# Hedgehog linear attention with a gated Mish layer on one core: one half-piece of w1, the kv product and Q's subtraction moved within the seven-product chunks

## The chip, the cores and the metric

The kernel runs on one NeuronCore of one Trainium2 chip. TensorE (PE) multiplies matrices, VectorE (DVE) does element work and reductions, ScalarE (ACT) does activations and copies, GpSimd (POOL) does element work and starts some DMAs, SyncE (SP) starts most of the others. Each engine runs its own instructions in order and waits on semaphores of the others. The metric is the device time of the program in microseconds (us).

## The reference, cut to what matters

```python
qkv = x @ wqkv                                   # x: 2048 x 512; q, k, v: 32 heads of 16
pq, pk = q @ w_phi, k @ w_phi                    # per head
phi = concat(softmax(p), softmax(-p))            # for q and k
kv, z = phi_k^T v, sum_s phi_k                   # per head
a = ((phi_q kv) / (phi_q z + 1e-6)) @ wo
b = mish(x @ w1 + b1) @ w2                       # 512 -> 1376 -> 512
out = g * a + (1 - g) * b,  g = sigmoid(x . gate_w)
```

## The kernel before

The 2048 rows of x are cut into eight chunks (0 to 7) of 256 rows, two tiles of 128 each. Phase A runs over the chunks and makes, for each tile t, K with w_phi folded in (`k`), V (`v`) and Q (`q`), the feature map E of K, and adds up kv = E^T v in one PSUM tile and z = sum of E. Q goes to DRAM (`pqd`) and is read again in phase B. Phase B then runs over four blocks of 512 rows: the Mish layer (`up`, `down`), Q's features, the numerator (`nu`), wo and the output.

Every float32 operand of a large product is split into a high part (an ACT copy to fp32r, step `H`, `xh`, `sh`) and a low part (a subtraction, step `O`, `xl`, `sl`), and a product is high*high + high*low + low*high. w1 and w2 are loaded and split in phase A in twelve numbered pieces, 1024 columns wide but for pieces 5 and 11 (512): `Lj` starts the load of piece j (line 165, on SP), `Hj` is ACT's copy, `Oj` POOL's subtraction (line 517). Raw pieces share two buffers, so `Lj` waits for the `O` two loads back: L5 for O3, L7 for O5, L8 for O11, L9 for O7.

A chunk as a rule takes 72 matmuls of 128x512. Chunks 3, 4 and 5 (`FAST`) take 66: K and Q of two tiles are a 2x2 block product, done with seven half-size products (`s1` to `s7`, six matmuls each) in place of eight, plus 24 matmuls for V. Their operands are combinations of x's blocks, made one chunk ahead: `sa` (four POOL additions, line 335), `sh0`/`sl0` (for s7 and s6) and `sh1`/`sl1` (for s5 and s3; lines 342 and 343). The tiles with the raw combinations are called sraw; their split parts lie for now in w2b's tiles, and the split combinations of the weights in w2a's and w2b's, so that w2ah or w2bh in the profile's "proj" products are these operands. In PE's order a chunk is s1, s7, s2, s6, v0, s4, s5, v1, s3. ACT copies s1's result into Q's PSUM tile (`bc`) and s7's into SBUF (`m7`). DVE adds them into the second K's PSUM tile (`ca`, line 381), upon which s4 accumulates; after s5, DVE subtracts the second tile's Q out of the same PSUM tile (`qa`, line 420), and only then may s3 go on accumulating there. qa's result goes to DRAM by `st1`.

The feature map of tile t on DVE: maxima and minima of each head (`mx`, `mn`, line 262), two subtractions (`d0`, `d1`, lines 269 and 271), ACT's exponential (`E`), sums (`S`, line 277), reciprocals (`rS`, line 285) and the scaling E*1/S (`ml`, line 293). Then E goes to `z` (chunks 0 to 4: an accumulating DMA that POOL starts, line 445; later an addition on POOL, line 443), and both tiles of two chunks go to kv together (`kk`, 64 small matmuls a chunk): chunks 2 and 3 in chunk 4's time, 4 and 5 in chunk 6's. `xh`, `xl` split the next chunk's x, `ldx` loads the one after that.

The order of all steps is written out by hand as strings of step names: `SEVEN` for chunks 3 to 5, `NEXT` for 6, `LAST` for 7, `BLOCK0` and on for phase B. `run` emits steps in that order, and each engine keeps the order in which its instructions are emitted. A trailing ' means the previous chunk's step, + the next one's, # a weight piece. In SEVEN the words `more` and `rest` stand for weight pieces and differ by chunk. POOL's `O` steps and the first addition of `sa` are made to wait for the DVE step emitted last, by hand:

```python
def behind(ins, other=None):
    tc.add_manual_dep(ins.ins, (other or dve[0]).ins.name, SYNC, reason="VectorE's step first")
...
            behind(pin(G_.tensor_sub(l[:, cs], raws[j], f32(h[:, cs]))))
```

where `dve[0]` is the last `xl` or `ml` so far.

Of the kernel before, what the change touches and what calls it, by code (L numbers as in the profile page):

```python
# [49 lines left out]
    v1 H1# S1 rS1 ml1 l3# O1# L3# ve1 q0 qe0 st0 q1 qe1 st1  # L50
"""
SEVEN = """
    s1 bc s7 m7 kk s2 xh xl zld sa z1' more mx0 mn0 s6 ca d00 d10 E0 ldx v0 ve0 sh0 sl0 za rest S0 rS0 s4 mx1 mn1 s5 qa st1 d01 d11 E1 ml0 z0
    v1 S1 rS1 s3 ve1 qe0 st0 ml1 sh1 sl1
"""
NEXT = """
    lq0+ k0 xh xl z1' mx0 mn0 k1 kk d00 d10 ldx H9# E0 O9# ldw0 L10# mx1 mn1 d01 d11 H6# E1 O6# ldw1 S0 rS0 ml0 z0 v0 ve0 H10#
# [37 lines left out]
def tile_gated_mix(ctx: ExitStack, tc: tile.TileContext, xT, wv, wkT, wqT, bd, w1a, w1b, b1, w2a, w2b, wo, out):  # L95
# [109 lines left out]
    def run(text, key, prev=None, nxt=None):  # L205
        for w in text.split():
            k = prev if w.endswith("'") else nxt if w.endswith("+") else "W" if w.endswith("#") else key
            for fn in steps.pop((k, w.rstrip("'+#")), ()):
                fn()
# [664 lines left out]
    run(SECOND, ("A", 1), ("A", 0))  # L874
    run(BEFORE, ("A", 2), ("A", 1))
    for c in FAST:
        w = {3: ("", "H2# O2# L4# H3# O3# L5#"), 4: ("", "H4# O4# L11# H5# O5# L7#"), 5: ("H11# O11# L8# H7# O7# L9#", "H8# O8# L6#")}[c]
        run(SEVEN.replace("more", w[0]).replace("rest", w[1]), ("A", c), ("A", c - 1))
    for c, text in ((NCH - 2, NEXT), (NCH - 1, LAST)):
        run(text, ("A", c), ("A", c - 1), ("B", 0))  # L880
    for b in range(NB):
# [62 lines left out]
```

## Time and profile before

| what | value |
|---|---|
| median of 3 runs | 453.68 us (449.16 to 454.94) |
| the profiled execution's own time | 454.35 us |
| its span in the profile | 452.3 us |
| PE busy / DVE busy / ACT / POOL | 442.9 / 318.9 / 209.4 / 161.9 us |
| chunk 3, from s1 to the next s1 | 64.81 to 80.45 us |
| chunk 4 | 80.45 to 101.77 us |
| chunk 5 | 101.77 to 116.73 us |
| phase B starts | 153.89 us |

The profile is of one execution; its times are counted from the start of the span. A row of the timeline gives the start, the length, the engine, the line of the code, the operation with the tile written and the tiles read, and in brackets the idle time of the engine ahead of it and what ended that. The own time is 2.05 us longer than the span, which is what lies around it.

### The profile page before, as it was taken

To read this page: it belongs to the slowest core of one execution; us is meant where nothing else is said; L and a number is where in the kernel's file an instruction comes from. 1 tells how busy PE (TensorE), PEld (TensorE's weight loads), DVE (VectorE), ACT (ScalarE), POOL (GpSimd) and SP (SyncE) were. 2 spreads that over 40 slices of the span, in tenths; PEclk is the share of its full clock that TensorE was granted. 3 is DMA by queue.
4 is the path that set the end of the run, shared out by engine and by line. 5 is a ranking of instruction groups with operands and counts; after the bars stand their busy time and mean duration, and the time that the engine had idled before them with its cause. 6 is when DMAs were issued, how large, how long until landed. Compare 5 with 4: busy or idle time off the path is not lost.

```text
span 452.3 us, 7013 instructions
## 1 busy us (share of the span) xinstructions
PE 442.9 (98%) x2754; PEld 361.3 (80%) x2754; DVE 318.9 (71%) x423; ACT 209.4 (46%) x289; POOL 161.9 (36%) x116
## 2 busy tenths in 40 slices
PE   7999999799999999999999999999999999999996
PEld 7888887688888888878787887887887888787885
DVE  2499778887899999799989976576967529611002
ACT  5774554445445565726265444534253553243220
POOL 2296757667495455221122212023212122221211
PEclk9999999999999999999999999999999999999999
DMA  7426756748955200413434150331151302030002
GB/s 279 164 82 203 162 113 166 185 100 224 275 201 154 73 24 1 99 43 87 146 94 141 30 156 32 92 112 47 30 136 58 94 13 93 1 84 11 0 0 93
DMA packets 27320, 46.35 MB, mean 102 GB/s; under 512 B 5908, under 2 KB 14100, under 8 KB 27288
## 3 DMA queue, kind: packets, MB, share of 16 engines
q1 hardware_dynamic: 25528, 39.88, 28.7%
q0 software_dynamic: 1616, 5.77, 6.7%
q8 instruction: 21, 0.34, 0.3%
q10 hardware_dynamic: 144, 0.26, 0.2%
q14 instruction: 11, 0.09, 0.1%
HBM read 23.87 MB, written 13.64 MB: 83 GB/s over the span
## 4 chain that ended last, share of the span: by engine, by line
PE 93%; DVE 4%; DMA 1%; issue 1%; ACT 0%; DVEq 0%; ACTq 0%
PE up L107 27%; PE down L107 26%; PE proj L107 25%; PE wo L107 10%; PE num L107 2%; PE fuse L107 2%; PE kvp L107 1%; DVE E L293 1%; DMA wT<-in_wkT_dram 1%; DVE Sm L277 1%; DVE io L788 0%; DVE mx L262 0%; DVE E L271 0%; DVE E L269 0%; DVE mn L262 0%
## 5 line engine op out<-in xcount | busy, mean ns | idle before, releaser
L653 POOL TENSOR_TENSOR l<-act,h 128x512 fp32r<-128x512 f32 x44 | 60.3, 1370 | 219.9 <-ACT h L127 184.2
L127 ACT ACTIVATE act<-up,b1s 128x512 f32<-128x512 f32 x44 | 30.3, 688 | 88.8 <-PE up L107 88.7
L127 ACT ACTIVATE E<-E 128x1024 f32<-128x1024 f32 x32 | 33.6, 1060 | 51.4 <-DVE E L271 31.2
L293 DVE TENSOR_TENSOR E<-E,Sm 128x1024 f32<-128x1024 f32 x32 | 46.4, 1451 | 1.0
L277 DVE TENSOR_REDUCE Sm<-E 128x64 f32<-128x1024 f32 x32 | 38.7, 1211 | 7.8 <-ACT E L127 7.8
L107 PE MATMUL wo<-woh,ohl 128*128 128x512 f32 x128 | 40.7, 389 | 0.0
L107 PE MATMUL down<-w2ah,h 128*128 128x512 f32 x96 | 37.5, 390 | 0.0
L107 PE MATMUL down<-w2ah,l 128*128 128x512 f32 x96 | 37.4, 389 | 0.0
L107 PE MATMUL down<-w2al,h 128*128 128x512 f32 x96 | 37.3, 389 | 0.0
L788 DVE SCALAR_TENSOR_TENSOR io<-down,og_sb,io 128x512 f32<-128x512 f32 x16 | 11.2, 749 | 31.0 <-PE down L107 31.0
L107 PE MATMUL down<-w2bh,h 128*128 128x512 f32 x80 | 31.2, 390 | 0.0
L107 PE MATMUL down<-w2bl,h 128*128 128x512 f32 x80 | 31.1, 389 | 0.0
L107 PE MATMUL down<-w2bh,l 128*128 128x512 f32 x80 | 31.1, 389 | 0.0
L127 ACT ACT_TABLE_LOAD x20 | 25.7, 1283 | 10.1 <-PE up L107 9.8
L762 DVE TENSOR_TENSOR ohl<-num,ohl 128x512 fp32r<-128x512 f32 x16 | 10.2, 679 | 26.3 <-ACT ohl L127 26.3
L127 ACT ACTIVATE h<-act 128x512 fp32r<-128x512 f32 x44 | 27.8, 632 | 1.4
L107 PEld LDWEIGHTS wo<-woh,ohl 128*128 128x128 f32 x128 | 24.0, 188 | 5.1
L107 PE MATMUL up<-xbh,w1ah 128*128 128x512 f32 x96 | 26.2, 394 | 0.0
L107 PE MATMUL up<-xbh,w1al 128*128 128x512 f32 x96 | 25.7, 389 | 0.0
L107 PE MATMUL up<-xbl,w1ah 128*128 128x512 f32 x96 | 25.7, 389 | 0.0
L107 PE MATMUL wo<-wol,ohl 128*128 128x512 f32 x64 | 24.9, 389 | 0.0
L550 DVE TENSOR_TENSOR xbl<-xraw,xbh 128x1024 fp32r<-128x1024 f32 x8 | 10.0, 1287 | 19.8 <-ACT xbh L127 19.8
(156 smaller groups left out, 1014.8 us busy)
## 6 DMA issues: line engine op xcount, KB each, us to landing
xraw<-in_xT_dram SPq DMA_DIRECT2D x16, 512.0 KB, 4.5
eT<-tt SPq DMA_DIRECT2D x128, 64.0 KB, 2.0
zd<-E POOLq DMA_DIRECT2D x10, 512.0 KB, 6.0
pqd<-qs SPq DMA_DIRECT2D x16, 256.0 KB, 4.0
pq<-pqd SPq DMA_DIRECT2D x16, 256.0 KB, 2.9
out_dram<-io SPq DMA_DIRECT2D x16, 256.0 KB, 2.1
raw<-in_w1a_dram SPq DMA_DIRECT2D x3, 512.0 KB, 4.5
raw<-in_w2a_dram SPq DMA_DIRECT2D x3, 512.0 KB, 4.2
```

Source lines behind the costliest of these rows:

```text
L107: return pin(nc.tensor.matmul(*a, **k))
L127: return pin(A_.activation(out_, in_, fn, **k))
L277: pin(V.tensor_reduce(d["S"], hv(d["E"][:, :]), axis=AX.X, op=ALU.add))
L293: dve[0] = pin(eng.tensor_mul(hv(d["E"][:, :]), hv(d["E"][:, :]), d["S"][:, :, None].to_broadcast([P, 2 * H, DH])))
L550: dve[0] = pin(V.tensor_sub(xb[b][1][:, :, sl], kt(raw[h], SC), f32(xb[b][0][:, :, sl])))
L653: pin(G_.tensor_sub(U[i]["l"], U[i]["a"], f32(U[i]["h"])))
L762: pin(V.tensor_sub(ohl[h, gp][:, 512:], num[h, gp], f32(ohl[h, gp][:, :512])))
L788: pin(V.scalar_tensor_tensor(io[t], dn[t], og_sb[:, i : i + 1], io[t], op0=ALU.mult, op1=ALU.add))
```

## The change

In the words of the strings: SEVEN's `kk` moves from behind m7 to behind s6 (it does something in chunk 4 alone); `qa st1` moves ahead of `mx1 mn1` in chunks 3, 4 and 5 (s5, a PE step, comes with it in the text, and PE's own order stays); and a new word `late` at the end of the string takes the second weight piece of the middle of the chunk: in chunk 3 `O3 L5`, in chunk 4 `O5 L7`, in chunk 5 nothing. H3 and H5, ACT's copies, stay where they were. Since `late` follows ml1, the DVE step that O3 and O5 wait for by hand is now ml1, the second scaling, and no longer the xl or ml0 of before. No instruction is added or taken away.

```diff
 SEVEN = """
-    s1 bc s7 m7 kk s2 xh xl zld sa z1' more mx0 mn0 s6 ca d00 d10 E0 ldx v0 ve0 sh0 sl0 za rest S0 rS0 s4 mx1 mn1 s5 qa st1 d01 d11 E1 ml0 z0
-    v1 S1 rS1 s3 ve1 qe0 st0 ml1 sh1 sl1
+    s1 bc s7 m7 s2 xh xl zld sa z1' more mx0 mn0 s6 kk ca d00 d10 E0 ldx v0 ve0 sh0 sl0 za rest S0 rS0 s4 s5 qa st1 mx1 mn1 d01 d11 E1 ml0 z0
+    v1 S1 rS1 s3 ve1 qe0 st0 ml1 sh1 sl1 late
 """
...
-        w = {3: ("", "H2# O2# L4# H3# O3# L5#"), 4: ("", "H4# O4# L11# H5# O5# L7#"), 5: ("H11# O11# L8# H7# O7# L9#", "H8# O8# L6#")}[c]
-        run(SEVEN.replace("more", w[0]).replace("rest", w[1]), ("A", c), ("A", c - 1))
+        w = {3: ("", "H2# O2# L4# H3#", "O3# L5#"), 4: ("", "H4# O4# L11# H5#", "O5# L7#"), 5: ("H11# O11# L8# H7# O7# L9#", "H8# O8# L6#", "")}[c]
+        for name, part in zip(("more", "rest", "late"), w):
+            text = (SEVEN if name == "more" else text).replace(name, part)
+        run(text, ("A", c), ("A", c - 1))
```

PE at the start of chunk 4, before: proj_870 is s7, kvp are the kv products of chunk 2 (E_608, E_641) and chunk 3 (E_778, E_833), proj_869 is s2, proj_877 is s6.

```order
L107 MATMUL proj_870<-w2ah_128,w2bl_131 128x512 x2
L107 MATMUL kvp_537<-E_608,v_668 32x64 x16
L107 MATMUL kvp_537<-E_641,v_694 32x64 x16
L107 MATMUL kvp_537<-E_778,v_797 32x64 x16
L107 MATMUL kvp_537<-E_833,v_861 32x64 x16
L107 MATMUL proj_869<-wkh_118,xh_753 128x512 x2
L107 MATMUL proj_869<-wkl_119,xh_753 128x512 x2
L107 MATMUL proj_869<-wkh_118,xl_755 128x512 x2
L107 MATMUL proj_877<-w2ah_128,w2bh_130 128x512 x2
```

And after, where E_830 is the second E of chunk 3 and proj_989 is v0:

```order
L107 MATMUL proj_869<-wkh_118,xl_755 128x512 x2
L107 MATMUL proj_877<-w2ah_128,w2bh_130 128x512 x2
L107 MATMUL proj_877<-w2al_129,w2bh_130 128x512 x2
L107 MATMUL proj_877<-w2ah_128,w2bl_131 128x512 x2
L107 MATMUL kvp_537<-E_608,v_668 32x64 x16
L107 MATMUL kvp_537<-E_641,v_694 32x64 x16
L107 MATMUL kvp_537<-E_778,v_797 32x64 x16
L107 MATMUL kvp_537<-E_830,v_858 32x64 x16
L107 MATMUL proj_989<-wvh_120,xh_752 128x512 x2
```

The 64 small products of kv (the profile counts two records for each) now stand behind s2 and s6.

POOL from the middle of chunk 3 to chunk 4's end, before: raw_692 is piece 3 (O3), raw_803 piece 4, raw_809 piece 5 (O5); w2bl is written by sl1, sl0 and sl1; zd are the accumulating DMAs; sraw_965<-xraw is sa.

```order
L517 TENSOR_TENSOR w1al_659<-raw_662,w1ah_658 128x1024
L517 TENSOR_TENSOR w1bl_806<-raw_692,w1bh_805 128x1024
L445 DMA zd_124<-E_778 128x1024
L343 TENSOR_TENSOR w2bl_131<-sraw_760,w2bh_130 128x512
L335 TENSOR_TENSOR sraw_965<-xraw_782 128x256 x2
L335 TENSOR_TENSOR sraw_965<-xraw_782,sraw_965 128x256 x2
L445 DMA zd_125<-E_833 128x1024
L343 TENSOR_TENSOR w2bl_131<-sraw_965,w2bh_130 128x512
L517 TENSOR_TENSOR w1bl_806<-raw_803,w1bh_805 128x1024
L517 TENSOR_TENSOR w1bl_806<-raw_809,w1bh_805 128x512
L445 DMA zd_124<-E_983 128x1024
L343 TENSOR_TENSOR w2bl_131<-sraw_965,w2bh_130 128x512
```

And after, where piece 5 is raw_867:

```order
L517 TENSOR_TENSOR w1al_659<-raw_662,w1ah_658 128x1024
L445 DMA zd_124<-E_778 128x1024
L343 TENSOR_TENSOR w2bl_131<-sraw_760,w2bh_130 128x512
L517 TENSOR_TENSOR w1bl_806<-raw_692,w1bh_805 128x1024
L335 TENSOR_TENSOR sraw_901<-xraw_782 128x256 x2
L335 TENSOR_TENSOR sraw_901<-xraw_782,sraw_901 128x256 x2
L445 DMA zd_125<-E_830 128x1024
L343 TENSOR_TENSOR w2bl_131<-sraw_901,w2bh_130 128x512
L517 TENSOR_TENSOR w1bl_806<-raw_803,w1bh_805 128x1024
L445 DMA zd_124<-E_983 128x1024
L343 TENSOR_TENSOR w2bl_131<-sraw_901,w2bh_130 128x512
L517 TENSOR_TENSOR w1bl_806<-raw_867,w1bh_805 128x512
```

O3 passed z's DMA and sl1 and stands right ahead of the next chunk's sa; O5 passed the same two.

SP over the same stretch and into chunk 5, before: raw_803 is L4, raw_809 L5, raw_1008 L11, raw_1012 L7, pqd the stores of Q, xraw_987 is ldx, zacc is zld.

```order
L165 DMA raw_803<-in_w1b_dram 128x1024
L165 DMA raw_809<-in_w1b_dram 128x512
L424 DMA pqd<-qs_830 128x512
L424 DMA pqd<-qs_863 128x512
L152 DMA xraw_987<-in_xT_dram 128x1024
L165 DMA raw_1008<-in_w2b_dram 128x512
L165 DMA raw_1012<-in_w2a_dram 128x1024
L424 DMA pqd<-qs_1033 128x512
L424 DMA pqd<-qs_1066 128x512
L453 DMA zacc_1104<-zd_124 128x1024
```

And after, where raw_867 is L5 and raw_1070 is L7:

```order
L165 DMA raw_803<-in_w1b_dram 128x1024
L424 DMA pqd<-qs_823 128x512
L424 DMA pqd<-qs_860 128x512
L165 DMA raw_867<-in_w1b_dram 128x512
L152 DMA xraw_987<-in_xT_dram 128x1024
L165 DMA raw_1008<-in_w2b_dram 128x512
L424 DMA pqd<-qs_1026 128x512
L424 DMA pqd<-qs_1063 128x512
L165 DMA raw_1070<-in_w2a_dram 128x1024
L453 DMA zacc_1104<-zd_124 128x1024
```

L5 and L7 went behind their chunk's two stores of Q, so that L7 stands right ahead of zld. On DVE the subtraction qa (qs<-proj,m) goes ahead of the second tile's two reductions in each of the three chunks.

## The prediction

> **What bounds the kernel now.** I read the page first, then PE's waits, then the timeline around the longest of them.
>
> ```profile
> span 452.3 us, 7013 instructions
> PE 442.9 (98%) x2754; PEld 361.3 (80%) x2754; DVE 318.9 (71%) x423; ACT 209.4 (46%) x289; POOL 161.9 (36%) x116
> PE 93%; DVE 4%; DMA 1%; issue 1%; ACT 0%; DVEq 0%; ACTq 0%
> ```
>
> PE is busy 98% of the span and carries 93% of the chain that ended last. A change that touches no PE instruction can only move PE's waits, and these are few:
>
> ```profile
> PE kvp L107 <- DVE E L293: 2.4, 1, 2.4
> ...
> PEld proj L107 <- DVE qs L420: 0.5, 1, 0.5
> ```
>
> The long one is kv in chunk 4, waiting for the scaling of chunk 3's second E. PE's rows there, a kv without a wait, and twelve matmuls at full clock from the chain of waits:
>
> ```profile
> 83.26 1.55 PE L107 MATMUL kvp<-E,v 128*32 128x64 f32 x96
> 87.23 0.65 PE L107 MATMUL kvp<-E,v 128*32 128x64 f32 x32 [2.43 <-DVE E L293]
> ...
> 92.25 1.07 PE L107 MATMUL proj<-wvh,xh 128*128 128x512 f32 x4
> ...
> 122.26 1.99 PE L107 MATMUL kvp<-E,v 128*32 128x64 f32 x128
> 124.18 1.20 PE L107 MATMUL proj<-wvh,xh 128*128 128x512 f32 x4
> ...
> 160.53 2.72 PE up L107 x12
> ...
> 85.00:90.00 5.00, 2.77 (x38) 2.28 (x39) 3.26 (x4) 0.00 (x1) 2.57 (x4) 0.83 0.89 193
> ```
>
> The wait costs more than its 2.43. From 87.23 to v0 at 92.25 pass 5.02 us. A quarter of kv is 1.92 / 4 = 0.48 (122.26 to 124.18), and s2 and s6 are twelve matmuls, 2.72: 3.20. The other 1.82 are the halved clock that the window shows (mean 0.83). So this place costs 2.43 + 1.82 = 4.25. Why was the scaling late?
>
> ```profile
> 77.08 0.63 DVE L262 TENSOR_REDUCE mx<-proj 128x32 f32<-128x512 f32 x1
> ...
> 77.67 2.40 POOL L517 TENSOR_TENSOR w1al<-raw,w1ah 128x1024 fp32r<-128x1024 f32 x1
> 78.21 0.68 DVE L420 SCALAR_TENSOR_TENSOR qs<-proj,m 128x512 f32<-128x512 f32 x1
> 80.01 3.52 DVE L293 TENSOR_TENSOR E<-E,Sm 128x1024 f32<-128x1024 f32 x1
> 80.02 2.41 POOL L517 TENSOR_TENSOR w1bl<-raw,w1bh 128x1024 fp32r<-128x1024 f32 x1
> 82.05 0.63 ACT L127 ACTIVATE w2bh<-sraw 128x512 fp32r<-128x512 f32 x1
> 83.44 1.21 DVE L277 TENSOR_REDUCE Sm<-E 128x64 f32<-128x1024 f32 x1
> 84.42 1.57 POOL L343 TENSOR_TENSOR w2bl<-sraw,w2bh 128x512 fp32r<-128x512 f32 x1
> 84.68 0.55 DVE L285 RECIPROCAL Sm<-Sm 128x64 f32<-128x64 f32 x1
> 85.27 1.82 DVE L293 TENSOR_TENSOR E<-E,Sm 128x1024 f32<-128x1024 f32 x1
> 87.01 1.28 DVE L254 TENSOR_TENSOR xl<-xraw,xh 128x512 fp32r<-128x512 f32 x2
> ```
>
> ml0 took 3.52 where ml1 of chunk 4 (below) takes 1.23: it ended 1.1 behind O3 (80.02 + 2.41 = 82.43), as if DVE's and POOL's two-input operations in SBUF took turns, O3 first. sl1 then held ml1 up by 0.6. Two operations that ask at once may go either way: below, at 129.73, DVE waits for one POOL operation and then goes ahead of the next.
>
> **The change, part by part.** *qa ahead of mx1 and mn1*: it takes mx1's place in chunk 3 and starts 1.13 earlier (77.08 for 78.21), so s3, which waited 0.54 for it, waits no more: -0.5. DVE's order of the rest and its sum are unchanged, E1 starts when it did; this costs nothing, since DVE does the same five operations in a row.
>
> *O3 behind ml1*: ml0 starts at 80.07, when O2 ends, and ends at 81.3. S1 and rS1 (1.2 and 0.6) bring ml1 to 83.1; sl1, behind sh1 (82.05 + 0.63), runs 82.7 to 84.3 at most, so ml1 ends by 85.5, not 87.09.
>
> *kv behind s6*: s1 of chunk 4 starts 0.5 earlier and kv at 83.26 - 0.54 + 2.72 = 85.4; its last quarter is due at 86.9 and ml1 ended at 85.5. The wait and the slow clock go: -4.25. PE is then 4.79 early. With nothing else, 454.35 - 4.79 = 449.6.
>
> But DVE and POOL are not 4.79 early, and what waits behind O3 and O5 is late. Behind O3 on POOL stands sa, behind L5 on SP ldx of chunk 6. O3 runs from 86.8 (behind xl, 85.5 to 86.8) to 89.2, sa to 92.1 where before it ended at 91.34; ldx moves by as much and is not wanted before xh, 9 us later: nothing. L5 lands before H5. Stores of Q only get earlier. mx0, mn0, ca end at 88.6, and s4 is due at 92.25 - 4.79 + 2.72 = 90.2: nothing. Rows of the rest:
>
> ```profile
> 89.80 1.54 POOL L335 TENSOR_TENSOR sraw<-xraw,sraw 128x256 f32<-128x256 f32 x2
> ...
> 102.55 0.33 SPq L165 DMA_DIRECT2D raw<-in_w2a_dram  x1
> 103.21 1.23 DVE L293 TENSOR_TENSOR E<-E,Sm 128x1024 f32<-128x1024 f32 x1
> ...
> 106.80 1.06 ACT L127 ACTIVATE w2ah<-raw 128x1024 fp32r<-128x1024 f32 x1
> ...
> 110.16 1.06 ACT L127 ACTIVATE E<-E 128x1024 f32<-128x1024 f32 x1 [2.30 <-DVE E L271]
> 110.49 0.43 SPq L165 DMA_DIRECT2D raw<-in_w2a_dram  x1
> ...
> 111.45 0.42 SPq L152 DMA_DIRECT2D xraw<-in_xT_dram  x1
> ...
> 114.11 0.68 DVE L420 SCALAR_TENSOR_TENSOR qs<-proj,m 128x512 f32<-128x512 f32 x1
> ...
> 115.37 0.62 PE L107 MATMUL proj<-wqh,w2bh 128*128 128x512 f32 x2
> ...
> 116.88 1.06 ACT L127 ACTIVATE w2ah<-raw 128x1024 fp32r<-128x1024 f32 x1 [5.18 <-DMA raw<-in_w2a_dram]
> ...
> 120.76 1.22 DVE L293 TENSOR_TENSOR E<-E,Sm 128x1024 f32<-128x1024 f32 x1
> ...
> 129.73 1.65 DVE L293 TENSOR_TENSOR E<-E,Sm 128x1024 f32<-128x1024 f32 x1
> 130.24 3.39 POOL L517 TENSOR_TENSOR w2al<-raw,w2ah 128x1024 fp32r<-128x1024 f32 x1
> ...
> 150.43 1.91 DVE L293 TENSOR_TENSOR E<-E,Sm 128x1024 f32<-128x1024 f32 x1
> ...
> 152.86 1.10 PE L107 MATMUL kvp<-E,v 128*32 128x64 f32 x64
> ...
> 122.00:152.00 30.00, 30.00 (x311) 24.71 (x310) 29.49 (x38) 15.87 (x20) 21.02 (x8) 1.00 0.50 166
> ```
>
> *O5 and L7 behind ml1 of chunk 4.* From sa at 92.1: sh0 and sl0 to 94.0, O4 (2.4) to 96.4. DVE goes on from ca (88.6): two subtractions, E0, S0, rS0 (1.3, 1.1, 1.2, 0.6) to 92.8, s5 ends at 92.9, and qa and four operations of 0.6 bring it to 96.1; O4 holds ml0 until 97.6. S1 and rS1 to 99.4; on ACT sh1 follows E1 (96.1 to 97.2), v1's copy and qe0 (0.5 each) to 98.8; sl1 holds the turn to 100.2, ml1 runs to 101.4 (before: 104.44). Then xl to 102.7, O5 (half a piece, 1.3) to 104.0, and only then L7 starts: 104.05, 1.5 later than before, while PE is 4.79 earlier. L7 was in use 106.80 - 102.55 = 4.25 after its issue. At that it lands at 108.3, H7 runs to 109.4, and E0 of chunk 5 stands behind H7 on ACT: 109.4 to 110.4. S0, rS0, qa follow (1.2, 0.6, 0.6) to 112.9. s3 of chunk 5 is due at 115.37 - 4.79 = 110.6. **PE waits 2.3 there: a new wait, of about the length of the old one.** Behind L7 on SP stand zld and L8, both still earlier than before (106.3 for L8's 110.49); behind L9, which waits for O7, ldx of chunk 7 at 112.3, 0.9 later than its 111.45; its x is wanted at 120.4, 8 us on.
>
> Does that wait halve the clock? The bounds are 0 and 1.82. Around the old wait PE did nothing but thin kv from 83.26 to 87.9, 4.6 us; the 1.92 us of thin kv at 122.26 was followed by full speed (124.18). 2.3 is nearer to 1.92: I take 0.
> The Trainium skill (TensorE: Matmul & The Clock Gate, Part 1) says that the clock halves after an idle window of about 3.4 us. By it a wait of 2.3 between dense matmuls costs nothing more, the sum that I take; the trace halves after a wait of 2.43, so the rule holds here only if thin kv counts as idle.
>
> Then k0, k1 and kk of chunk 6: kk is due at 122.26 - 4.79 + 2.3 = 119.8. DVE goes on from qa (112.9) through four operations to 115.3. L8 at 106.3 with its 6.39 from before (116.88 - 110.49) gives H8 at 112.7, O8 from 113.8 to 116.2, and ml0 behind it ends at 117.4; S1, rS1 and ml1 (1.2, 0.6, 1.2) end at 120.4 (before 120.76 + 1.22 = 121.98); kk's last quarter is due at 121.2: no wait. From 122 to 152 DVE is busy 29.49 of 30 us, so that ml1 of chunk 7, which ended at 150.43 + 1.91 = 152.34, comes 1.6 earlier too, at 150.7; kv's second half is due at 152.86 - 2.5 + 0.5 = 150.9. It fits by 0.2.
>
> **Sum:** 454.35 - 0.54 - 4.25 + 2.3 = 451.9. That is against the profiled execution's own time, 0.67 above the median of 453.68. The run of 449.16 lies near my 449.6, so perhaps O3 lost its turn there and the old wait was absent.
>
> **Rivals.** *All of it is kept*: 449.6. L7 would have to be in use 2.3 sooner; against it, a wait of a whole xl, O5 and load stands ahead of H7.
>
> *Turns are lost, or the clock halves*: O3 or O5 may go between the two xl and hold the second up 2.4 or 1.3; ca of chunks 4 and 5 is then late, or the additions to zacc on POOL fall on xl of chunk 7. The clock would add 1.82: 453.7. With DVE a whole POOL operation (2.4) late at 150.7, kv of chunk 7 waits 2.2: 454.1. The turn at 80.01 speaks for it, that at 129.73 against. In all 453 to 454.5, as good as no change.
>
> *Slower, by L7's load*: zld is issued right behind L7 and the z DMA beside it. L8, issued in such company, took the 6.39 above. If L7 takes that, s3 waits 2.3 + 2.14 = 4.4, and the clock falls for 1.82: 449.6 + 6.2 = 455.8. It decides from a wait of 4.79 - 1.82 = 3.0, a load of 5.0. Against it: L7 had a z DMA beside it before and took 4.25.
>
> **How the numbers follow.** The forecast, 451.9 (450.4 to 453), has a chance of 0.43; all kept, 0.17; turns or clock, 0.27; slower by L7, 0.13. The range, 449.3 to 455.2, takes in the first three and the near end of the last. About 2% is what a measurement of this kernel tells from no change, that is 9 us: faster needs more than all of PE's waits in phase A, 0.01; slower needs two stalls like the worst rival, 0.02; within, 0.97.
>
> **What would show it.** In the profile after: ml0 of chunk 3 at 1.2 to 1.3 and not 3.52; no wait of kv in chunk 4 and a clock of 1.00 at 85 to 95; s3 of chunk 3 without a wait; O3 at about 87; L7 issued near 104, H7 waiting for its DMA, E0 of chunk 5 behind it, and PE waiting about 2.3 for qa (line 420) in chunk 5. No such wait would make the forecast wrong towards 449.6; a wait of over 3 with a slow clock, or waits at s4, towards 454 and beyond.

## The result and the profile after

| kernel | median of its runs, us | lowest and highest | runs |
|---|---|---|---|
| before, beside the change | 450.27 | 449.16, 454.94 | 20 |
| after | 453.48 | 452.68, 456.62 | 20 |

The ratio of after to before is 1.0067, with a 95% interval of 1.0045 to 1.0089: beside these runs of before the change costs about 3 us, where the prediction expected a gain of about 2 (from 453.68 to 451.9). Its 451.9 is 1.6 too low, and its direction is wrong.

The runs of before fall into two groups with a gap between them. Of the 20, 16 lie from 449.16 to 451.18 (median 450.09) and 4 from 453.06 to 454.94 (median 454.12). The profile that the prediction was worked out from, 454.35, is of the upper group, which is the rarer one here. Of the 20 runs of the change, 18 lie from 452.68 to 454.46; the other two, at 456.58 and 456.62, have a mean granted clock of 0.996 where the 18 have 0.998 to 1.00. By the medians the change lies 3.4 above before's lower group and 0.6 below the upper. How large its loss against before as a whole is depends on how many of before's runs are in each group.

The profiled execution of after took 453.54. From its page, the span and the busy times; PE is busy for as large a share as before, and DVE for 6 us more:

```profile
span 451.6 us, 7015 instructions
PE 441.9 (98%) x2754; PEld 359.5 (80%) x2754; DVE 324.9 (72%) x423; ACT 209.0 (46%) x289; POOL 158.5 (35%) x116
```

PE's waits, in total, times and longest. The 2.4 at kv and the 0.5 at s3 are gone, and there are others:

```profile
PE kvp L107 <- DVE E L293: 1.6, 1, 1.6
...
PE proj L107 <- ACT proj L127: 0.4, 1, 0.4
...
PE proj L107 <- DVE qs L420: 0.4, 1, 0.4
...
PE proj L107 <- DVE proj L381: 0.3, 1, 0.3
```

Chunk 3's end and chunk 4's start, from the timeline (start, length, engine, line, operation, tiles, and in brackets the idle time ahead and what ended it):

```profile
76.68 0.63 DVE L420 SCALAR_TENSOR_TENSOR qs<-proj,m 128x512 f32<-128x512 f32 x1
...
78.27 0.61 PE L107 MATMUL proj<-wqh,w2bh 128*128 128x512 f32 x2
...
79.74 1.22 DVE L293 TENSOR_TENSOR E<-E,Sm 128x1024 f32<-128x1024 f32 x1
...
82.80 2.07 DVE L293 TENSOR_TENSOR E<-E,Sm 128x1024 f32<-128x1024 f32 x1
...
82.95 0.74 PE L107 MATMUL proj<-wkh,xh 128*128 128x512 f32 x2 [0.44 <-ACT proj L127]
...
84.78 3.48 DVE L254 TENSOR_TENSOR xl<-xraw,xh 128x512 fp32r<-128x512 f32 x2
84.94 2.78 POOL L517 TENSOR_TENSOR w1bl<-raw,w1bh 128x1024 fp32r<-128x1024 f32 x1 [1.17 <-DVE E L293]
85.94 1.99 PE L107 MATMUL kvp<-E,v 128*32 128x64 f32 x128
...
87.86 1.20 PE L107 MATMUL proj<-wvh,xh 128*128 128x512 f32 x4
```

The same stretch as a window, PE's busy time ahead and the granted clock in the third place from the end:

```profile
85.00:90.00 5.00, 5.00 (x142) 4.12 (x141) 5.00 (x6) 0.00 (x0) 4.32 (x4) 1.00 0.64 157
```

The old stall is gone, as foretold: s3 (78.27) doesn't wait, ml0 of chunk 3 takes 1.22 and not 3.52, kv (85.94) runs in one piece, and the clock is 1.00. Two rows are new. s2 (82.95) waits 0.44 for ACT's `bc`; before, kv stood ahead of it. And O3 (84.94) got in between the two `xl`, which take 3.48 where in the profile of 454.35 they took 1.28.

The weights' path from O5 to s3 of chunk 5:

```profile
102.27 2.38 DVE L254 TENSOR_TENSOR xl<-xraw,xh 128x512 fp32r<-128x512 f32 x2
102.42 1.67 POOL L517 TENSOR_TENSOR w1bl<-raw,w1bh 128x512 fp32r<-128x512 f32 x1 [1.16 <-DVE E L293]
...
104.12 0.33 SPq L165 DMA_DIRECT2D raw<-in_w2a_dram  x1
...
106.50 0.72 PE L107 MATMUL proj<-w2bh,xh 128*128 128x512 f32 x2 [0.34 <-DVE proj L381]
...
108.23 1.06 ACT L127 ACTIVATE w2ah<-raw 128x1024 fp32r<-128x1024 f32 x1 [5.64 <-DMA raw<-in_w2a_dram]
...
109.20 1.05 ACT L127 ACTIVATE E<-E 128x1024 f32<-128x1024 f32 x1
...
112.00 0.63 DVE L420 SCALAR_TENSOR_TENSOR qs<-proj,m 128x512 f32<-128x512 f32 x1
...
112.68 0.73 PE L107 MATMUL proj<-wqh,w2bh 128*128 128x512 f32 x2 [0.43 <-DVE qs L420]
```

L7 is issued at 104.12 (prediction: 104.05), ACT is idle for 5.64 ahead of H7 until its load is there, E0 stands behind H7 and s3 waits for `qa`: the predicted chain, row for row. That the time of L7 fits within 0.1 is luck: ml1 of chunk 4 ended at 102.35 and not at 101.4, and O5 did not wait for both `xl`, as predicted, but went between them. Then chunk 6's start and kv of chunk 7:

```profile
119.64 1.23 DVE L293 TENSOR_TENSOR E<-E,Sm 128x1024 f32<-128x1024 f32 x1
119.71 1.99 PE L107 MATMUL kvp<-E,v 128*32 128x64 f32 x128
120.78 3.48 DVE L254 TENSOR_TENSOR xl<-xraw,xh 128x512 fp32r<-128x512 f32 x2
120.92 2.79 POOL L443 TENSOR_TENSOR zacc<-zacc,E 128x1024 f32<-128x1024 f32 x1 [4.12 <-DVE E L293]
...
150.31 0.65 PE L107 MATMUL kvp<-E,v 128*32 128x64 f32 x32
150.54 1.91 DVE L293 TENSOR_TENSOR E<-E,Sm 128x1024 f32<-128x1024 f32 x1
...
152.60 0.65 PE L107 MATMUL kvp<-E,v 128*32 128x64 f32 x32 [1.63 <-DVE E L293]
```

An addition to zacc on POOL (120.92) got in between the two `xl` of chunk 7, which takes 2.2 of DVE's time (3.48 for 1.28). DVE has next to no slack from there on (busy 29.72 of the 30 us from 122 to 152), and the last quarter of kv waits 1.63 at 152.60 for ml1 of chunk 7.

### The profile page after: what moved, and what is told of

It reads as the page before. It is cut to its first block, busy times and chain, and to the rows that moved or that the text cites. A ratio compares the mean times of both kernels' runs of the same rounds, so it can differ in the third digit from the quotient of the medians.

```text
span 451.6 us, 7015 instructions
## 1 busy us (share of the span) xinstructions
PE 441.9 (98%) x2754; PEld 359.5 (80%) x2754; DVE 324.9 (72%) x423; ACT 209.0 (46%) x289; POOL 158.5 (35%) x116
## 4 chain that ended last, share of the span: by engine, by line
PE 65%; DVE 6%; issue 0%
PE up L107 27%; PE down L107 26%; PE wo L107 10%; PE num L107 2%; DVE E L293 2%; DVE Sm L277 1%; DVE E L269 1%; DVE mx L262 1%; DVE E L271 1%; DVE Sm L285 0%; DVE io L788 0%; DVE mn L262 0%; PE z L107 0%; PE kvp L107 0%; PE kvT L607 0%
```

## The experiments

Below, a place is counted from v0 of chunk 4, the last step at which after and before's lower group are level (87.86 and 87.89 from the span's start). s3 of chunk 5 in after, for example, is at 112.68 - 87.86 = 24.82. "up" is the first product of phase B behind kv of chunk 7. All are starts of PE's rows in the timeline.

| kernel (median, us) | s2, chunk 5 | s4, chunk 5 | s3, chunk 5 | kk, chunk 6 | up |
|---|---|---|---|---|---|
| before, profile of 454.35 | 12.24 | 17.68 | 23.12 | 30.01 | 61.64 |
| before, profile of 450.01 | 12.24 | 17.68 | 23.12 | 30.01 | 61.64 |
| after (453.48) | 12.57 | 18.64 | 24.82 | 31.85 | 65.32 |
| O3 late alone (451.11) | 12.24 | 17.68 | 23.16 | 30.22 | 61.85 |
| O5 late alone (454.06) | 12.24 | 17.68 | 24.69 | 31.72 | 64.05 |
| all but O5's move (450.82) | 12.60 | 18.33 | 23.92 | 30.82 | 62.45 |
| after, z0 behind xl (452.45) | 12.60 | 18.67 | 24.77 | 31.81 | 64.15 |
| after, H7 behind E0 (454.18) | 12.60 | 18.67 | 24.26 | 31.16 | 65.59 |
| O3 behind xl, kv and qa moved (450.36) | 12.37 | 17.81 | 23.25 | 30.14 | 61.77 |

From v0 of chunk 4 on, the two profiles of before read alike: what tells them apart lies ahead of it. From s1 of chunk 3 to v0 of chunk 4 they take 27.44 and 23.35, which are 4.09 of the 4.34 between their times. After takes 23.45 there, no less than the lower group.

**Before, once more.** No edit: the profile of a run of the lower group was wanted.

> The kernel before, unchanged, for a second profile of it. Its 20 runs have a median of 450.27 and four near or over 453, and the profile shown is one of these four. If the long wait of kv in chunk 4 is what sets the four apart, an execution near 450 shows it gone or under 1 us, the clock at 1.00 from 85 to 95, and ml0 of chunk 3 at 1.2 to 1.3 us in place of 3.52. If all executions of before have that wait, one near 450 shows it too, and gains its 4 us elsewhere.

It took 450.01, and its profile is of the lower group. ml0 and O3 ask within 0.01 again, and this time ml0 goes first and O3 waits:

```profile
79.73 1.22 DVE L293 TENSOR_TENSOR E<-E,Sm 128x1024 f32<-128x1024 f32 x1
79.74 3.46 POOL L517 TENSOR_TENSOR w1bl<-raw,w1bh 128x1024 fp32r<-128x1024 f32 x1
...
83.02 2.08 PE L107 MATMUL kvp<-E,v 128*32 128x64 f32 x128
...
111.01 0.61 PE L107 MATMUL proj<-wqh,w2bh 128*128 128x512 f32 x2
...
117.39 1.29 DVE L254 TENSOR_TENSOR xl<-xraw,xh 128x512 fp32r<-128x512 f32 x2
...
117.90 1.99 PE L107 MATMUL kvp<-E,v 128*32 128x64 f32 x128
...
148.50 1.10 PE L107 MATMUL kvp<-E,v 128*32 128x64 f32 x64
```

kv runs without a wait, and so do s3 of chunk 5 and kv of chunk 7. A run in which ml0 gets the turn pays nothing of the 4.25 that the change was to remove.

**One piece at a time.** The change moves two subtractions of weight pieces: O3, of a piece of 1024 columns, and O5, of the half-piece that the title names. Here are O3 late alone, O5 late alone, and all of the change but O5. The first two keep kv and qa where before has them:

```diff
-    v1 S1 rS1 s3 ve1 qe0 st0 ml1 sh1 sl1
+    v1 S1 rS1 s3 ve1 qe0 st0 ml1 sh1 sl1 late
...
+        w = {3: ("", "H2# O2# L4# H3#", "O3# L5#"), 4: ("", "H4# O4# L11# H5# O5# L7#"), ...
...
+        w = {3: ("", "H2# O2# L4# H3# O3# L5#"), 4: ("", "H4# O4# L11# H5#", "O5# L7#"), ...
```

> Before, with O3 and L5 alone at the end of chunk 3. Theory A (the price is O5 and L7, which come late and hold up E0 of chunk 5): nothing is paid here, 449 to 450.5, ratio 0.997 to 1.001. Rival B (the price is O3, which now takes a turn between the two xl of chunk 4 and delays DVE by 2.2 us): most of the loss is here already, 452.5 to 454, ratio 1.005 or more.

> Before, with O5 and L7 alone at the end of chunk 4. Theory A: H7 waits for its load, E0 of chunk 5 comes behind it, DVE and then PE are late: 452 to 454, ratio 1.005 to 1.008. Rival B: no loss, 449.5 to 450.5, ratio 0.998 to 1.001.

> The change without its part in chunk 4: kv behind s6, Q's subtraction ahead, O3 and L5 late, O5 and L7 where they were. Theory A: the wait of kv is gone in all executions and nothing is paid, 449 to 450, ratio 0.995 to 0.999. Rival B: as slow as the whole change, 452.5 to 454, ratio 1.005 or more.

Before's median beside them was 453.55, since 19 of its 29 runs fell into the upper group (one of them, 451.82, lies between the groups). O3 late alone: 451.11 (450.06 to 452.73), ratio 0.9973 (0.9945 to 1.0001). This is above Theory A's 449 to 450.5 and below Rival B's 452.5 to 454; kv, which stays behind s7, still waits 0.45 for ml1 in its profile. O5 late alone: 454.06, in two groups, 451.53 to 453.27 and 454.85 to 456.65, as before's but 2 to 3 us higher: 1.0048 (1.0012 to 1.0084). Its profile is of the lower of its groups, and it shows both of the late places, s3 of chunk 5 and the `xl` of chunk 7:

```profile
113.10 0.73 PE L107 MATMUL proj<-wqh,w2bh 128*128 128x512 f32 x2 [1.33 <-DVE qs L420]
...
120.04 3.48 DVE L254 TENSOR_TENSOR xl<-xraw,xh 128x512 fp32r<-128x512 f32 x2
```

All but O5: 450.82 (449.62 to 451.98), 0.9955 (0.9931 to 0.998), which is 0.8 above the 450 that Theory A allowed at most, with the two `xl` of chunk 7 undisturbed:

```profile
85.16 3.48 DVE L254 TENSOR_TENSOR xl<-xraw,xh 128x512 fp32r<-128x512 f32 x2
...
118.56 1.29 DVE L254 TENSOR_TENSOR xl<-xraw,xh 128x512 fp32r<-128x512 f32 x2
```

O3's meeting with `xl` is there too (3.48), and by the table this kernel loses 0.81 by kk of chunk 6, against 1.84 for after, and nothing more at kv of chunk 7. O5 late alone loses 1.71 by kk and 2.41 in all. So the larger part of the price is O5's and L7's, by both paths: at s3 of chunk 5 and at kv of chunk 7. That O3 between the `xl` is the main price is refuted.

**Four on one chip: the change again, two mends of it, and another place for O3.** In the first mend the first addition of chunk 5's E to zacc stands behind `xl` of chunk 7, in the second H7 stands behind E0 and v0's copy on ACT; in the last kernel kv and qa are moved as in the change, O5 stays, and O3 stands behind both `xl`, ahead of `sa`. The first two edits are against after, the last one against before:

```diff
-    lq0+ k0 xh xl z1' mx0 mn0 k1 kk ...
+    lq0+ k0 xh xl z0' z1' mx0 mn0 k1 kk ...
...
-5: ("H11# O11# L8# H7# O7# L9#", "H8# O8# L6#", "")
+5: ("H11# O11# L8#", "H7# O7# L9# H8# O8# L6#", "")
...
+        w = {3: ("", "H2# O2# L4# H3#"), 4: ("", "H4# O4# L11# H5# O5# L7#"), ...
+        run(SEVEN.replace("sa z1'", "O3# L5# sa z1'" if c == 4 else "sa z1'") ...
```

> The change itself, on one chip with the three kernels below. Theory A (the price is that s3 of chunk 5 waits about 1.9 us longer than in the fast mode of before, because H7 stands behind L7's late load and E0 behind H7, and that kv of chunk 7 waits 1.6 because an addition to zacc goes between the two xl of chunk 7): 453.0 to 454.0, without the two modes of before, s3 at 112.7 and kv's last quarter at 152.6 as in its first profile. Rival B (the difference to before lies in which mode before's runs fall into on a chip, and the change itself also has two modes): its runs spread over 450 to 455 like those of before.

> The change, with the first addition of chunk 5's E to zacc moved on POOL behind xl of chunk 7. Theory A: the two xl of chunk 7 take about 1.3 and not 3.48, DVE is 2.2 earlier from there on, kv of chunk 7 no longer waits 1.63 for its scaling, and the time is 1.3 to 1.7 below the change's: about 452. Rival (DVE's 2.2 are given back to POOL at another place before 150, or the addition now takes the turn of another DVE operation): xl short, kv's wait still 1 or more, the time within 0.5 of the change's.

> The change, with H7, O7 and L9 taken in chunk 5 behind E0, v0's copy and za; L7 stays late. Theory A: E0 of chunk 5 goes to ACT at about 107 and not 109.2, s3 of chunk 5 is at 111 instead of 112.7, kk of chunk 6 at 118; 1.5 to 1.9 less than the change, 451.5 to 452, if the wait of kv in chunk 7 stays, and 450.2 if it goes too. L9 and ldx behind it come 2 later; if x of chunk 7 is then late, some of it is given back. Rival (E0 is held by the subtractions on DVE and not by H7): E0 within 0.5 of 109.2 and the time that of the change.

> Before with the moves of kv and of qa, with O3 and L5 behind both xl of chunk 4 (ahead of sa), and O5 and L7 where before has them. Theory A: O3 meets neither ml0 nor xl, L7 is early, so no wait of PE over 0.5 in phase A: 449 to 450.5, in one mode. Rival C (moving O3 behind xl delays sa, and with it sh0, s6 and s7 of the next chunk, or ldx): PE waits at s7 or s6 of chunk 5, 451 to 453.

Before's median was 453.38 (16 runs in the lower group, median 449.76, and 19 in the upper, median 453.9; one of the 19, 452.02, lies between the groups).

*The change again*: 453.76 (451.93 to 454.25), not spread like before's, and counted from v0 of chunk 4 the same places as in its first profile (s3 at 24.87 for 24.82, up at 65.42 for 65.32). It is 4.0 above before's lower group here, but since more than half of before's runs are in the upper one, its ratio to before is 1.0027 (0.9998 to 1.0057): on this chip no loss against before as a whole is shown.

*z0 behind `xl`*: 452.45 (451.6 to 453.67), 1.3 below the change, ratio to before 0.9991 (0.9962 to 1.0021).

```profile
121.64 1.28 DVE L254 TENSOR_TENSOR xl<-xraw,xh 128x512 fp32r<-128x512 f32 x2
...
123.01 4.89 POOL L443 TENSOR_TENSOR zacc<-zacc,E 128x1024 f32<-128x1024 f32 x2 [5.34 <-DVE xl L254]
...
152.05 0.65 PE L107 MATMUL kvp<-E,v 128*32 128x64 f32 x32 [0.21 <-DVE E L293]
```

`xl` is back to 1.28 and kv's wait to 0.21. This shows that the addition in the gap of `xl` makes most of what is lost at kv of chunk 7: by the table, from kk of chunk 6 to "up", 1.13 of after's 1.84. What makes the other 0.71 no run shows. The addition in this gap need not cost as much: in O5 late alone it takes the same gap (3.48 at 120.04), DVE reaches these `xl` 1.29 earlier, counted from v0 of chunk 4, and the loss there is 0.70.

*H7 behind E0*: 454.18 (453.73 to 456.51), ratio 1.0055 (1.0022 to 1.0087), not the 450.2 to 452 that the theory gave.

```profile
108.04 1.06 ACT L127 ACTIVATE E<-E 128x1024 f32<-128x1024 f32 x1 [5.11 <-DVE E L271]
...
112.47 0.62 PE L107 MATMUL proj<-wqh,w2bh 128*128 128x512 f32 x2
...
113.62 5.10 POOL L517 TENSOR_TENSOR w2al<-raw,w2ah 128x1024 fp32r<-128x1024 f32 x2
...
113.92 5.88 DVE L293 TENSOR_TENSOR E<-E,Sm 128x1024 f32<-128x1024 f32 x1
...
123.48 0.66 PE L107 MATMUL kvp<-E,v 128*32 128x64 f32 x32 [2.57 <-DVE E L293]
```

E0 starts when its subtractions are done and s3 no longer waits for `qa`, so H7 did hold them up. But of s3's 1.70 this takes back 0.56 only (24.26 for 24.82): 0.99 were lost by s4 already, which H7 doesn't touch. That H7's hold is enough by itself for nearly all of the 1.70 is shown by O5 late alone: nothing is lost there up to s4 (17.68), and s3 is 1.57 late (24.69). And the late load comes back in another place: O7 and O8 now run back to back on POOL (5.10), ml0 of chunk 5 waits for both (5.88, ending 1.08 behind them), and the last quarter of kv in chunk 6 waits 2.57. The `xl` of chunk 7 take 1.28 here, and kv there doesn't wait.

*O3 behind `xl`*: 450.36 (449.4 to 451.28), one group, ratio 0.9954 (0.9924 to 0.9984), 3.4 below the change on the same chip.

```profile
83.39 0.73 PE L107 MATMUL proj<-wkh,xh 128*128 128x512 f32 x2 [0.41 <-ACT proj L127]
...
85.22 1.28 DVE L254 TENSOR_TENSOR xl<-xraw,xh 128x512 fp32r<-128x512 f32 x2
...
86.33 1.99 PE L107 MATMUL kvp<-E,v 128*32 128x64 f32 x128
86.58 2.39 POOL L517 TENSOR_TENSOR w1bl<-raw,w1bh 128x1024 fp32r<-128x1024 f32 x1 [2.37 <-DVE xl L254]
```

O3 meets neither ml0 nor `xl`. Its one wait is again s2's for `bc` (0.41). The rival, a late `sa`, didn't show.

**What makes the two groups, and what each move is worth.** kv's move alone; qa's alone; O3 behind `xl` alone; and O3 behind `xl` with kv's move, without qa's:

```diff
-    s1 bc s7 m7 kk s2 xh xl zld sa z1' more mx0 mn0 s6 ca ...
+    s1 bc s7 m7 s2 xh xl zld sa z1' more mx0 mn0 s6 kk ca ...
...
- ... s4 mx1 mn1 s5 qa st1 d01 d11 ...
+ ... s4 s5 qa st1 mx1 mn1 d01 d11 ...
```

> Before with kv alone moved behind s6. Lottery theory (before's runs form two groups, near 449.8 and near 453.9, because at about 80 either ml0 or O3 goes first, and where O3 does, kv of chunk 4 waits 2.43 and the clock halves for 1.82): kv's last quarter is now due at about 87.4, ml1 ends at 87.1 at the latest, so no wait and no slow clock whoever goes first; the group at 454 disappears, all runs lie from 449.3 to 451.5. Rival (the two groups have another cause, a load or the chip): two groups, 4 apart, remain.

> Before with qa and its store alone moved ahead of the second K's maxima. Lottery theory: the turn at 80 is untouched, so two groups as in before, the upper one 0.5 lower at most, since s3 of chunk 3 no longer waits 0.54: 449.8 and 453.4. Rival (qa's place decides how ml0 and O3 meet, since DVE is 0.6 earlier or later there): one group only, and the profile shows ml0 and O3 apart.

> Before with O3 and L5 alone moved behind both xl of chunk 4; kv and qa stay. Lottery theory: ml0 has POOL off its way in every run, ml1 ends in time for kv in chunk 4: 449.5 to 450.5 in one group, without kv's moving. Rival: kv, which stays behind s7, still waits up to 1 for ml1 (it ends at about 84.5), and the time is 450.5 to 451.5.

> As the kernel with O3 behind xl, kv and qa moved, which took 450.36, but with qa where before has it. It tells what qa's move is worth. If it gains the 0.54 that s3 of chunk 3 waited: 450.9. If it costs, since in chunk 4 qa waits 1.56 for s5 and holds up the second K's maxima behind it: 449.5 to 450.1. If neither: 450.4.

Before's median beside them, on another chip, was 451.35 (19 runs from 448.88 to 451.39, 16 from 452.75 to 455.54).

| kernel | median | lowest and highest | ratio, interval |
|---|---|---|---|
| kv alone | 450.45 | 450.07, 451.64 | 0.9964, 0.9936 to 0.9992 |
| qa alone | 453.79 | 452.84, 454.76 | 1.0042, 1.0012 to 1.0072 |
| O3 behind xl alone | 450.32 | 449.6, 451.09 | 0.9953, 0.9922 to 0.9984 |
| O3 behind xl, kv | 450.06 | 449.39, 450.93 | 0.995, 0.992 to 0.9979 |

None has two groups. With kv behind s6 or O3 out of ml0's way, the upper group is gone, as the theory of the turn at 80 said. The rival for O3 behind `xl` alone was right about the wait, not about the time: kv still waits 0.47 for ml1 in its profile, and the median is 450.32. qa's move alone went against the theory, which had foretold two groups: all twelve runs lie in the upper one. Its timeline, the turn and the wait:

```profile
80.27 2.41 POOL L517 TENSOR_TENSOR w1bl<-raw,w1bh 128x1024 fp32r<-128x1024 f32 x1
80.39 3.38 DVE L293 TENSOR_TENSOR E<-E,Sm 128x1024 f32<-128x1024 f32 x1
...
87.48 0.65 PE L107 MATMUL kvp<-E,v 128*32 128x64 f32 x32 [2.85 <-DVE E L293]
```

And its window around that wait, the granted clock third from the end:

```profile
86.00:92.00 6.00, 4.52 (x49) 3.81 (x50) 4.71 (x7) 0.00 (x0) 3.50 (x6) 1.00 0.59 112
```

With qa ahead of the maxima, DVE comes to ml0 0.12 behind POOL, where in both profiles of before it came 0.01 ahead, and by the twelve times O3 has the turn in every run. So the rival holds in that qa's place decides who goes first, and not in that the two stay apart. The Trainium skill (SBUF — State Buffer, "SBUF: two separate sides") says that VectorE with two inputs in SBUF and GpSimd share a pair of ports, and that whoever starts first holds it for the whole instruction. The rows agree where the starts are apart: with 0.12 between them, ml0 waits out O3's 2.41. With 0.01 between them it went either way, and in before's second profile it is O3 that waits (3.46).

qa's move on top of the other two is worth nothing that shows: 450.36 with it, 450.06 without, on different chips. What s3 gains (s1 of chunk 4 comes 15.23 behind s1 of chunk 3 with it, for 15.64 in before's lower group) goes into s2's wait of 0.41 for `bc`, since that copy on ACT doesn't come earlier (17.87 behind s1 of chunk 3, for 17.75).

O3 behind `xl` with kv's move has the lowest median, 0.995 of before as a whole (0.992 to 0.9979); kv alone and O3 behind `xl` alone lie within 0.4 of it, with intervals that overlap. It is level with before's lower group (450.06 beside 450.08), and gains by being there in every run.

## Why the prediction was wrong

- **The base of the sum** is the step that failed first: "So this place costs 2.43 + 1.82 = 4.25", taken off as if every run of before paid it. It is the price of one outcome of a race between ml0 and O3, and by their times 4 of the 20 runs beside the change paid it. The prediction saw the sign, "perhaps O3 lost its turn there and the old wait was absent", and did not draw the conclusion: then before's usual time is about 450, and whatever the change adds is a loss. Its own terms on that base, 449.6 + 2.3 = 451.9, already were a slowdown against the median of 450.27. So the 449.6 was near the truth (the lower group's median is 450.09), and what was wrong is that most of before's runs were there already.
- **kv of chunk 7, "It fits by 0.2"**, is the second step that failed. The addition to zacc took the gap between the two `xl` of chunk 7. That was in the rival on lost turns (454.1 for a whole POOL operation; chance 0.27 with the clock), in whose 453 to 454.5 the measured 453.48 lies. PE waits 1.63 there and is 1.84 later up to phase B; taking the addition away gave back 1.13 of that in the profile, and 1.3 of the median.
- **"O3 runs from 86.8 (behind xl, ...)"** was wrong in place: `behind` ties O3 to ml1, not to `xl`, so it went between them at 84.94 and made `xl` 3.48. Alone this costs nothing from v0 of chunk 4 to s4 of chunk 5 (17.68); with kv's and qa's moves the loss is 0.81 by kk of chunk 6, of which O3 behind `xl` with the same two moves shows 0.13 (30.14) as well.
- **qa, "this costs nothing"**: s3's wait went, as said, but s2 then waits 0.44, and alone the move hands O3 the turn. So from s1 of chunk 3 to v0 of chunk 4 the change is 3.99 shorter than the profile of 454.35 (23.45 for 27.44), where 4.79 was predicted.
- **kv behind s6**: right. No wait, no slow clock. That move or O3's by itself removes the upper group; the change has both.
- **L7, H7, E0, s3**: the chain was right, and its size too large: 1.70 late at s3 where 2.3 was predicted. In the change not all of it hangs on H7's hold on E0, since part is lost ahead of s3 as well. 0.33 is lost at s2, and 0.63 at s4, which waits for `ca`; ahead of `ca` on DVE the `xl` took 2.38, with O5 in their gap. The clock stayed at 1.00, as taken. That kk of chunk 6 is at 119.71 for a predicted 119.8 is luck: less was gained ahead of v0 of chunk 4 than predicted, less was lost behind it, and this run reached chunk 3 at 64.41 for 64.81.
- **The sum as measured**: the lower group's 450.09, less 0.03 at v0 of chunk 4, plus 1.84 by kk of chunk 6, plus 1.84 at kv of chunk 7: 453.7, where 453.48 was measured.
- **Slower by L7's load**: ACT was idle for 5.64 ahead of H7, but the load was in use 4.1 after its issue (108.23 - 104.12), as assumed. The rival did not occur.

What stays open is why the share of before's runs in the upper group moves between sets of runs: 4 of 20, and in the three later sets 19 of 29, 19 of 35 and 16 of 35; and what makes the 0.71 at kv of chunk 7 that are left without the addition.

## What to carry to other kernels

Before a stall is counted as a gain, ask whether every run pays it: where two engines ask for the same turn within some hundredths of a microsecond and the few times shown spread by 1%, one profile shows one outcome. Where POOL's operation and DVE's take turns, moving one behind a later step of the other engine helps only if that step is not followed at once by another of the same kind; otherwise it lands in the gap between them. And a step that frees a buffer drags its load along, with all that stands behind the load's user: here moving the half-piece of w1 alone (O5 late) made one exponential late, s3 of chunk 5 behind it by 1.57, and kv of the last chunk.

## What was not expected of the hardware

- Two operations of DVE back to back are not one for the turn: POOL's operation, asked for 0.14 to 0.16 after the first of two `xl` began, ran between them, three times in after (84.94, 102.42 and 120.92). The other way round it went both ways: at 129.73 in before DVE waited for one operation of POOL and went ahead of the next, while with H7 behind E0 two of POOL's ran back to back (5.10), and DVE's ml0, which started 0.3 after the first, waited for both.
- A tenth of a microsecond decides over 3 to 4. In before ml0 and O3 start 0.01 apart, and the runs split; with 0.12 between them in the one profile of qa's move, all twelve times are in the upper group.
- The length of PE's wait doesn't decide on the clock. After 2.43 of waiting at kv of chunk 4 the window of 86 to 92 in before shows a clock of 0.72; after 2.85 at the same place with qa moved alone, the same window above shows 1.00, so the sum's 1.82 wasn't sure even in the upper group. In that same profile a wait of 2.11 ahead of 6.16 was followed by a clock of 0.50 from 8 to 10. The Trainium skill (TensorE: Matmul & The Clock Gate, Part 1) says that the window in which activity is watched runs freely. That would make it a matter of where the wait falls; the cases here do not show more than that the length alone isn't it.
